# State read-out by matmuls of 65 columns, out of a copy of x with ones between pairs of tiles

## The chip, the cores and the metric

The kernel runs on one core of a Trainium2 chip. The core has five engines with queues of their own: TensorE (PE, matrix multiply, writes to PSUM), VectorE (DVE), ScalarE (ACT), GpSimd (POOL, which also issues DMAs) and SyncE (SP, DMAs only). The metric is device time in microseconds; before the change it is 156.49 us, the median of 6 runs (155.84 to 157.29).

## What is computed

x is (8 batches, 8 heads, 512 positions, 64), state is (8, 8, 32, 64). Two attentions are read in both directions, joined, and put through a feed-forward layer that takes the largest of three products:

```python
scores = scale * x @ state.T;   a  = softmax(scores);   xread = a @ state      # 512 x 64 per head
scores2 = scale * state @ x.T;  a2 = softmax(scores2);  sread = a2 @ x         # 32 x 64 per head
y = concatenate([xread, sread], axis=2)                  # (8, 8, 544, 64)
y = y.transpose(0, 2, 1, 3).reshape(8 * 544, 512)
h = maximum(maximum(y @ w1, y @ w2), y @ w3)             # 4352 x 768
out = h @ w_out                                          # 4352 x 512, float32
```

The softmax subtracts the row's largest score in the reference; the kernel leaves that out. scores2 is the transpose of scores, so one exponential `e` serves both directions: `a` is `e` divided by its sums over the 32 states, and sread is e.T @ x divided by the sums of `e` over the 512 positions.

## The kernel before

All data is bfloat16 on chip, sums are float32 in PSUM. A batch's 512 positions lie on 128 partitions with J = 4 positions each, so that `x_sb[b]` is [128, 8 heads x 4 x 64] and, before the change, has 64 further columns that GpSimd sets to one (lines 66, 114 and 441).

For each batch there are these steps. `x_transpose` or `x_transpose_dma` turns x over (TensorE for batches 0 to 2, DMA transposes issued by SP for 3 to 7). `scores` (L196) multiplies it by a block-diagonal form of the states, and ScalarE's exponential gives `e` (L201). `softmax` sums and inverts on VectorE (L209, L211) and multiplies on GpSimd (L216) to give `a`, which is turned over again into `aT` (SP's DMA transpose, L232, from batch 3). `g_front` and `g_back` (L276) multiply the states by the weights w1, w2, w3 into `G`. `x_maxout` (L348 for the matmuls, L352 to L356 for ScalarE's copy and VectorE's two maxima) makes h from `G` and `aT`, and `ffn_out` (L386) multiplies by w_out; ScalarE copies to `osb` (L389) and GpSimd issues the output DMA in two halves (L400).

`sread(b)` is 32 matmuls (L246), for each of 4 positions j, 2 head groups g and 4 heads s. The stationary operand is a [128, 32] slice of `e`, the moving one has 128 columns: 64 of x and then the 64 columns of ones, one access pattern with a jump (L244). The four s go to four 32-column tiles of the array, which write four groups of 32 PSUM partitions. The result, [128, 2, 2, 64] in one PSUM bank, holds the weighted sums and 64 equal copies of the sum of `e`. VectorE takes the reciprocal of one of the copies (L251) and multiplies (L253) into `sr`; SP transposes that by DMA into `ats` later (L254), for the states' own maxout behind the last batch.

PSUM is held by two rings: "two" (two buffers of two banks: pg pieces and ps) and "pw" (four buffers of one bank: pw, po, psr, pgs and others). Each engine works strictly in the order in which the kernel's text gives it instructions; there is no scheduler. Batches 0 and 1 and part of 2 are written out by hand. From then on one loop pass per b (2 to 7) has six slots, one after each of the six `x_maxout(b, m)`, and the steps of the next batch n = b + 1 are spread over them:

```python
            slots[1].append(lambda: softmax(n, 0, 2, (nc.gpsimd.tensor_mul, J)))
            slots[2].append(lambda: a_transpose_dma(n))
        ...
            slots[4].append(lambda: sread(n))
            slots[4].append(lambda: g_front(n))
```

`ffn_out(b - 1, j)` stands in slots 1, 2, 4 and 5; in slot 4 it comes ahead of sread. sread(2) stands in the part by hand, between `ffn_out(0, 1)` and `g_front(2)`.

Of the kernel before, what the change touches and what calls it, by code (L numbers as in the profile page):

```python
# [8 lines left out]
F32 = mybir.dt.float32  # L9
BF16 = mybir.dt.bfloat16  # L10
AX = mybir.AxisListType
# [4 lines left out]
def kernel(  # L16
# [14 lines left out]
    nc = tc.nc  # L31

    B, H, S, D = x.shape
# [8 lines left out]
    J = 4  # L42
    HS = H // 2
    NM = d_ff // 128
    XW = H * J * D
# [3 lines left out]
    data = ctx.enter_context(tc.tile_pool(name="data", bufs=1))  # L49
    wpool = ctx.enter_context(tc.tile_pool(name="weights", bufs=1))  # L50
    work = ctx.enter_context(tc.tile_pool(name="work", bufs=2))
    pp = ctx.enter_context(tc.tile_pool(name="pp", bufs=2, space=bass.MemoryType.PSUM))
# [10 lines left out]
    load_st(0, nc.sync)  # L63


    x_sb = [data.tile([128, XW + D], BF16, name=f"x{b}") for b in range(B)]
    xv = [t[:, 0:XW].rearrange("p (h j d) -> p h j d", j=J, d=D) for t in x_sb]

    def load_x(b):
        nc.gpsimd.dma_start(  # L70
            out=x_sb[b][:, 0:XW].rearrange("p (h jd) -> p h jd", h=H),
            in_=x[b].rearrange("h (p j) d -> p h (j d)", j=J))
# [26 lines left out]
    def m_cols(t, m):  # L99
        c = [m0 <= m < m1 for m0, m1 in chunks].index(True)  # L100
        f = (m - chunks[c][0]) * 128
        return w_slices(t, c)[:, :, :, f:f + 128]
# [31 lines left out]
    def states_cast(k, cast):  # L134
        cast(out=st[k], in_=st_f[k].unsqueeze(2).to_broadcast((128, 4, 2, D)))
# [19 lines left out]
    def states(k, copy):  # L155
        states_transpose(k, False)
        states_place(k, copy)


    xT, e, a, aT, G, ht, osb = {}, {}, {}, {}, {}, {}, {}  # L160

    def new(d, b, shape, name, bufs=2):
        d[b] = work.tile(shape, BF16, tag=name, bufs=bufs, name=name)
# [16 lines left out]
    def x_transpose_dma(b):  # L180
        new(xT, b, [128, H, 2, 128], "xT", bufs=3)
        nc.sync.dma_start_transpose(out=xT[b].rearrange("p h j t -> p (h j) t"), in_=x_sb[b][:, 0:XW])

    def scores(b, g0, g1):
        n = g1 - g0
        if g0 == 0:
            new(e, b, [128, J, 2, HS, Ns], "e")
        if n == 2:
            p = pp.tile([128, J, n, HS, Ns], F32, tag="two", name="ps")
        else:  # L190
            p = pp.tile([128, J, n, HS, Ns], F32, tag="pw", bufs=4, name="psh")
        for jj in range(2):
            for g in range(g0, g1):
                for s in range(HS):
                    h = 2 * s + g
                    nc.tensor.matmul(  # L196
                        p[:, 2 * jj:2 * jj + 2, g - g0, s, :], xT[b][:, h, jj, :],
                        bd(b, h).rearrange("p c n -> p (c n)"),
                        start=(g == g0 and s == 0 and (n == 2 or jj == 0)),
                        stop=(g == g1 - 1 and s == HS - 1), skip_group_check=True)  # L200
        nc.scalar.activation(out=e[b][:, :, g0:g1], in_=p, func=AF.Exp, scale=scale)  # L201

    def softmax(b, g0, g1, *parts):

        n = g1 - g0
        if g0 == 0:
            new(a, b, [128, J, 2, HS, Ns], "a")
        den = work.tile([128, J, n, HS], F32, tag=f"den{n}", name="den")
        nc.vector.reduce_sum(out=den, in_=e[b][:, :, g0:g1], axis=AX.X)  # L209
        rden = work.tile([128, J, n, HS], F32, tag=f"rden{n}", name="rden")  # L210
        nc.vector.reciprocal(out=rden, in_=den)  # L211
        j0 = 0
        for mul, nj in parts:
            r = slice(j0, j0 + nj)
            j0 += nj
            mul(  # L216
                out=a[b][:, r, g0:g1].rearrange("p j g s n -> p j (g s) n"),
                in0=e[b][:, r, g0:g1].rearrange("p j g s n -> p j (g s) n"),
                in1=rden[:, r].rearrange("p j g s -> p j (g s)").unsqueeze(3).to_broadcast((128, nj, n * HS, Ns)))
# [10 lines left out]
    def a_transpose_dma(b):  # L230
        new(aT, b, [128, J, 2, 128], "aT", bufs=3)
        nc.sync.dma_start_transpose(  # L232
            out=aT[b].rearrange("p j g t -> p (j g) t"), in_=a[b].rearrange("p j g s n -> p (j g s n)"))

    late = []

    def sread(b):

        p = pp.tile([128, 2, 2, D], F32, tag="pw", bufs=4, name="psr")
        for j in range(J):  # L240
            for g in range(2):
                for s in range(HS):
                    xj = xv[b][:, 2 * s + g, j, :]
                    both = bass.AP(xj.tensor, xj.offset,  # L244
                                   (xj.ap[0], (XW - ((2 * s + g) * J + j) * D, 2), (1, D)))
                    nc.tensor.matmul(  # L246
                        p[32 * s:32 * s + 32, g], e[b][:, j, g, s, :], both,
                        start=(j == 0 and g == 0), stop=(j == J - 1), skip_group_check=True,
                        tile_position=(0, 32 * s))
        rd = work.tile([128, 2, 1], F32, tag="rd", name="rd")  # L250
        nc.vector.reciprocal(out=rd, in_=p[:, :, 1, 0:1])  # L251
        sr = work.tile([128, 2, D], BF16, tag="sr", bufs=B, name="sr")
        nc.vector.tensor_mul(out=sr, in0=p[:, :, 0, :], in1=rd.to_broadcast((128, 2, D)))  # L253
        late.append(lambda: nc.sync.dma_start_transpose(  # L254
            out=ats[:, b].rearrange("p s n -> p (s n)"), in_=sr.rearrange("p g d -> p (g d)")))

# [58 lines left out]
    def g_front(b):  # L315
        flush_copies()
        g_piece(b, 0, 512, act)
        g_piece(b, 512, 1024, act, True)
        g_piece(b, 1024, 1280, dve)

    def g_back(b):
        flush_copies()
        g_piece(b, 1280, 1792, act)
        g_piece(b, 1792, 2304, act, True)
# [16 lines left out]
    def maxout(b, m, n, lhs, rhs, nk):  # L341
        if m == 0:
            new(ht, b, [128, NM, n], "ht", bufs=4)
        pw = []
        for i in range(3):
            p = pp.tile([128, 512], F32, tag="pw", bufs=4, name=f"pw{i}")
            for k in range(nk):
                nc.tensor.matmul(p[:, 0:n], lhs(i, k), rhs(k), start=(k == 0), stop=(k == nk - 1))  # L348
            pw.append(p)
        t0 = work.tile([128, 512], BF16, tag="t0", name="t0")  # L350
        t1 = work.tile([128, 512], BF16, tag="t1", name="t1")
        nc.scalar.copy(out=t0[:, 0:n], in_=pw[0][:, 0:n])  # L352
        if copies_due:
            copies_due.pop(0)()
        nc.vector.tensor_max(t1[:, 0:n], t0[:, 0:n], pw[1][:, 0:n])  # L355
        nc.vector.tensor_max(ht[b][:, m, :], t1[:, 0:n], pw[2][:, 0:n])  # L356

    def x_maxout(b, m):
        maxout(b, m, 512,
               lambda i, k: m_cols(G[b], m)[:, k, i],  # L360
               lambda k: aT[b][:, :, k, :], 2)

    def s_maxout(m):
        maxout("s", m, B * Ns,
               lambda i, k: m_cols(w_sb, m)[:, k, i],
               lambda k: ats[:, :, k, :], HS)
# [70 lines left out]
        load_st(k, nc.gpsimd)  # L437
    load_x(3)
    load_x(4)
    for b in range(2, B):  # L440
        nc.gpsimd.memset(x_sb[b][:, XW:XW + D], 1.0)
    for k in range(1, B // 2):
        nc.gpsimd.memset(bds[k], 0.0)
    g_cols(0, (1,))
# [14 lines left out]
    x_maxout(1, 2)  # L459
    for k in range(1, B // 2):  # L460
        states_cast(k, pool)
    x_maxout(0, 4)
    states(1, act)
    x_transpose(2, 0, dve)
# [27 lines left out]
    for b in range(2, B):  # L492
        n = b + 1
        slots = [[] for _ in range(NM)]
        if n < B:
            slots[0].append(lambda: scores(n, 0, 2))
            slots[1].append(lambda: softmax(n, 0, 2, (nc.gpsimd.tensor_mul, J)))
            slots[2].append(lambda: a_transpose_dma(n))
            if n + 2 < B:
                slots[2].append(lambda: x_transpose_dma(n + 2))  # L500
            slots[5].append(late_transposes)
            if n + 3 < B:
                slots[0].append(lambda: load_x(n + 3))
        else:
            for m in range(NM):
                slots[m].append(lambda m=m: s_maxout(m))
        slots[1].append(lambda: g_back(b))
        if n < B:
            slots[4].append(lambda: sread(n))
            slots[4].append(lambda: g_front(n))  # L510
        for j, m in enumerate((1, 2, 4, 5)):
            slots[m].insert(0 if m > 2 else len(slots[m]), lambda j=j: ffn_out(b - 1, j))
        for m in range(NM):
            x_maxout(b, m)
            for f in slots[m]:
                f()
# [36 lines left out]
```

## Time and profile before

| what | value |
|---|---|
| median of 6 runs | 156.49 us (155.84 to 157.29) |
| the profiled execution's own time | 156.25 us |
| its span, first to last instruction | 154.4 us |
| TensorE busy, its granted clock | 147.1 us (95%), 1.00 |
| VectorE, ScalarE, GpSimd busy | 96.3, 94.8, 54.3 us |
| sread matmuls (L246) | 256, of 128 columns, in eight bursts of 32 |
| reciprocal L251, multiply L253 | 161 and 292 ns each, 8 of each |

A row of the groups reads: line, engine, operation, what it writes and reads, shapes, count, then busy us and mean ns of one, then the engine's idle time just before them and what ended it. A timeline or chain line begins with start and length in us, and ends with a count where equal instructions are merged. Busy times of TensorE overlap: a matmul's bar is its latency (219 ns for 128 columns), and the distance from one start to the next is what it costs in a stream.

### The profile page before, as it was taken

How to read it: one execution, taken by the hardware profiler on the slowest of the kernel's cores; microseconds unless marked ns; L12 is line 12 of the kernel's file. 1: busy time of each engine (PE TensorE's matmuls, PEld its weight loads, DVE VectorE, ACT ScalarE, POOL GpSimd, SP SyncE). 2: the span in 40 equal slices, each digit the busy share in tenths (PEclk: the TensorE clock that was granted, in tenths of full speed). 3: DMA queues.
4: the chain of work that ended last, by engine and by line, in shares of the span. 5: the costliest groups of instructions: out<-in, count | busy, mean ns of one | idle time of the engine just before them, and what ended most of it. 6: DMA issues, size and time to landing. Idle time of an engine off the chain costs nothing.

```text
span 154.4 us, 3492 instructions
## 1 busy us (share of the span) xinstructions
PE 147.1 (95%) x1390; PEld 71.9 (47%) x1390; DVE 96.3 (62%) x171; ACT 94.8 (61%) x147; POOL 54.3 (35%) x77
## 2 busy tenths in 40 slices
PE   6899899999999999999999999999999999999980
PEld 2456333454453445344534453445444655566440
DVE  3488776858637666766676667666766675565010
ACT  3667678885768566856685668566856555433350
POOL 8989989023990603060106010601060100101050
PEclk9999999999999999999999999999999999999999
DMA  4999999999699994959511961162115210300465
GB/s 113 219 183 171 177 213 202 236 188 177 89 150 339 203 270 118 149 115 248 119 63 36 225 164 63 66 152 81 59 70 142 84 56 0 138 0 0 185 198 165
DMA packets 36736, 21.72 MB, mean 141 GB/s; under 512 B 21968, under 2 KB 34384, under 8 KB 36720
## 3 DMA queue, kind: packets, MB, share of 16 engines
q0 software_dynamic: 17232, 15.08, 50.1%
q1 hardware_dynamic: 19344, 6.29, 21.9%
q8 instruction: 11, 0.18, 0.5%
q10 hardware_dynamic: 144, 0.13, 0.2%
q14 instruction: 5, 0.04, 0.1%
HBM read 15.20 MB, written 8.91 MB: 156 GB/s over the span
## 4 chain that ended last, share of the span: by engine, by line
PE 87%; DVE 5%; DMA 3%; ACT 1%; issue 1%; SPq 0%; DVEq 0%
PE pw L348 43%; PE po L386 28%; PE pg L276 4%; DMA x0f<-in_x_dram 3%; PE psr L246 2%; PE pxt L174 2%; PE ps L196 2%; PE idle L126 1%; DVE ht L356 1%; DVE t L355 1%; PE pg L302 1%; PE ph L378 1%; ACT t L352 1%; PE psh L196 1%; DVE xT L178 0%
## 5 line engine op out<-in xcount | busy, mean ns | idle before, releaser
L348 PE MATMUL pw<-aT,G 128*128 128x512 bf16 x288 | 69.5, 380 | 0.8 <-DVE sr L253 0.4
L355 DVE TENSOR_TENSOR t<-t,pw 128x512 bf16<-128x512 bf16 (+1 forms) x54 | 35.0, 649 | 30.5 <-ACT t L352 30.5
L386 PE MATMUL po<-wout,ht 128*128 128x512 bf16 x198 | 47.4, 380 | 0.2 <-DVE t L355 0.2
L348 PEld LDWEIGHTS <-G 128*128 128x128 bf16 x288 | 26.8, 98 | 33.3 <-issue 3.8
L356 DVE TENSOR_TENSOR ht<-t,pw 128x512 bf16<-128x512 bf16 (+1 forms) x54 | 35.6, 659 | 5.6
L389 ACT COPY osb<-po 128x512 f32<-128x512 f32 x33 | 19.2, 585 | 29.7 <-PE po L386 28.1
L352 ACT CAST t<-pw 128x512 bf16<-128x512 f32 (+1 forms) x54 | 30.5, 566 | 8.9 <-PE pw L348 7.9
L386 PEld LDWEIGHTS <-ht 128*128 128x128 bf16 x198 | 18.8, 98 | 23.9 <-issue 2.8
L400 POOL DMA_DIRECT2D out_dram<-osb x14 | 7.8, 560 | 55.3 <-ACT osb L389 45.9
L283 ACT CAST G<-pg 128x1024 bf16<-128x1024 f32 x24 | 24.5, 1022 | 3.6 <-PE pg L276 3.1
L216 POOL TENSOR_TENSOR a<-e,rden 128x1024 bf16<-128x1024 bf16 (+2 forms) x10 | 15.3, 1536 | 29.5 <-ACT t L352 15.4
L209 DVE TENSOR_REDUCE den<-e 128x32 f32<-128x1024 bf16 (+1 forms) x10 | 9.9, 995 | 0.7 <-ACT e L201 0.7
L308 ACT CAST G<-pg 128x768 bf16<-128x768 f32 x11 | 8.7, 810 | 2.0 <-PE pg L302 1.9
L109 POOL DMA_DIRECT2D w<-in_moe_w_dram x12 | 9.0, 787 | 0.0
L348 PE MATMUL pw<-ats,w 128*128 128x256 bf16 x72 | 8.8, 273 | 0.0
L201 ACT ACTIVATE e<-ps 128x1024 bf16<-128x1024 f32 x6 | 6.2, 1031 | 3.7 <-PE ps L196 3.7
L348 PEld LDWEIGHTS <-w 128*128 128x128 bf16 x72 | 7.0, 98 | 2.1
L276 PE MATMUL pg<-w,bd 64*32 64x512 bf16 x192 | 7.5, 382 | 0.0
L126 PE MATMUL idle<-zero 128*128 128x512 bf16 x20 | 6.2, 451 | 1.2 <-DVE zero L85 1.2
L196 PEld LDWEIGHTS <-xT 128*128 128x128 bf16 x128 | 5.0, 98 | 2.2 <-DVE xT L178 0.2
L70 POOL DMA_DIRECT2D x<-in_x_dram x6 | 5.4, 908 | 0.8 <-DMA w<-in_moe_w_dram 0.7
L286 DVE CAST G<-pgs 128x256 bf16<-128x256 f32 x12 | 4.5, 419 | 1.1 <-PE pgs L276 1.1
(55 smaller groups left out, 82.7 us busy)
## 6 DMA issues: line engine op xcount, KB each, us to landing
out_dram<-osb POOLq DMA_DIRECT2D x14, 512.0 KB, 3.5
x<-in_x_dram POOLq DMA_DIRECT2D x6, 512.0 KB, 8.9
w<-in_moe_w_dram POOLq DMA_DIRECT2D x6, 256.0 KB, 7.2
x<-in_x_dram POOLq DMA_DIRECT2D x3, 256.0 KB, 5.4
w<-in_moe_w_dram POOLq DMA_DIRECT2D x6, 128.0 KB, 5.8
wout<-in_moe_w_out_dram POOLq DMA_DIRECT2D x1, 768.0 KB, 11.3
x0f<-in_x_dram SPq DMA_DIRECT2D x1, 512.0 KB, 3.9
out_dram<-osb SPq DMA_DIRECT2D x1, 512.0 KB, 2.6
```

The costliest lines, as they stand in the source:

```text
L109: nc.gpsimd.dma_start(out=w_slices(w_sb, c)[:, :, i, :], in_=w[:, :, m0 * 128:m1 * 128])
L196: nc.tensor.matmul(p[:, 2 * jj:2 * jj + 2, g - g0, s, :], xT[b][:, h, jj, :], bd(b, h).rearrange("p c n -> p (c n)"), start=(g == g0 and s ...
L209: nc.vector.reduce_sum(out=den, in_=e[b][:, :, g0:g1], axis=AX.X)
L216: mul(out=a[b][:, r, g0:g1].rearrange("p j g s n -> p j (g s) n"), in0=e[b][:, r, g0:g1].rearrange("p j g s n -> p j (g s) n"), in1=rden[: ...
L276: nc.tensor.matmul(ps[g][32 * s:32 * s + 32], bd(b, 2 * s + g)[64 * g:64 * g + 64, g, :], w_sb[64 * g:64 * g + 64, s, c0:c1], start=True, ...
L283: copy(out=G[b][:, :, c0:c1], in_=p[:, :, 0:n])
L348: nc.tensor.matmul(p[:, 0:n], lhs(i, k), rhs(k), start=(k == 0), stop=(k == nk - 1))
L352: nc.scalar.copy(out=t0[:, 0:n], in_=pw[0][:, 0:n])
L355: nc.vector.tensor_max(t1[:, 0:n], t0[:, 0:n], pw[1][:, 0:n])
L356: nc.vector.tensor_max(ht[b][:, m, :], t1[:, 0:n], pw[2][:, 0:n])
L386: nc.tensor.matmul(p, ht[b][:, m, j * 128:(j + 1) * 128], wout_sb[:, m, :], start=(m == 0), stop=(m == NM - 1))
L389: act(out=o[:, j, :], in_=p)
```

## The change

For batches 2 to 7 sread reads another layout. Two buffers `x_pads` hold, for each pair of 64-wide tiles (one head, two positions j), two ones and then the pair's 128 columns, 130 in all, with two more ones at the very end. The ones are set once. `x_pad(b)` is one GpSimd copy of all of x's 2048 columns into buffer b % 2. It is issued for batch 2 after the states' casts in the part by hand, and for n = b + 1 in slot 1 behind the softmax of n.

A matmul now moves 65 columns. For even j it is one of the ones and the first tile of a pair, into PSUM columns 0 to 64; for odd j it is the second tile and the following one, into columns 1 to 65. So x's sums fall on columns 1 to 64 for both, and the sum of `e` comes in two parts, in columns 0 and 65, which VectorE adds with a reduce ahead of the reciprocal. The slices for even j begin at an odd element. Batches 0 and 1 keep the 128 columns. The ones behind x_sb[2] to x_sb[7], and the six memsets that made them, are gone.

```diff
-    x_sb = [data.tile([128, XW + D], BF16, name=f"x{b}") for b in range(B)]
+    x_sb = [data.tile([128, XW + D if b < 2 else XW], BF16, name=f"x{b}") for b in range(B)]
...
+    PW = 2 * D + 2
+    x_pads = [data.tile([128, (2 * H + 1) * PW], BF16, name=f"xp{k}") for k in range(2)]
+
+    def x_pad(b):
+        nc.gpsimd.tensor_copy(
+            out=x_pads[b % 2][:, 2:2 + 2 * H * PW].rearrange("p (k c) -> p k c", c=PW)[:, :, 0:2 * D],
+            in_=x_sb[b][:, 0:XW].rearrange("p (k c) -> p k c", c=2 * D))
+
     def sread(b):
-        p = pp.tile([128, 2, 2, D], F32, tag="pw", bufs=4, name="psr")
+        padded = b >= 2
+        p = pp.tile([128, 2, 2 * D], F32, tag="pw", bufs=4, name="psr")
         for j in range(J):
             for g in range(2):
                 for s in range(HS):
-                    xj = xv[b][:, 2 * s + g, j, :]
-                    both = bass.AP(xj.tensor, xj.offset,
-                                   (xj.ap[0], (XW - ((2 * s + g) * J + j) * D, 2), (1, D)))
+                    h = 2 * s + g
+                    if padded:
+                        c0 = (2 * h + j // 2) * PW + 1 + (D + 1) * (j % 2)
+                        cols = x_pads[b % 2][:, c0:c0 + D + 1]
+                        c = slice(j % 2, D + 1 + j % 2)
+                    else:
+                        xj = xv[b][:, h, j, :]
+                        cols = bass.AP(xj.tensor, xj.offset, (xj.ap[0], (XW - (h * J + j) * D, 2), (1, D)))
+                        c = slice(0, 2 * D)
                     nc.tensor.matmul(
-                        p[32 * s:32 * s + 32, g], e[b][:, j, g, s, :], both,
+                        p[32 * s:32 * s + 32, g, c], e[b][:, j, g, s, :], cols,
                         start=(j == 0 and g == 0), stop=(j == J - 1), skip_group_check=True,
                         tile_position=(0, 32 * s))
+        den, c = p[:, :, D:D + 1], slice(0, D)
+        if padded:
+            den, c = work.tile([128, 2, 1], F32, tag="rs", name="rs"), slice(1, D + 1)
+            nc.vector.reduce_sum(out=den, in_=p[:, :, 0:D + 2:D + 1], axis=AX.X)
         rd = work.tile([128, 2, 1], F32, tag="rd", name="rd")
-        nc.vector.reciprocal(out=rd, in_=p[:, :, 1, 0:1])
+        nc.vector.reciprocal(out=rd, in_=den)
         sr = work.tile([128, 2, D], BF16, tag="sr", bufs=B, name="sr")
-        nc.vector.tensor_mul(out=sr, in0=p[:, :, 0, :], in1=rd.to_broadcast((128, 2, D)))
+        nc.vector.tensor_mul(out=sr, in0=p[:, :, c], in1=rd.to_broadcast((128, 2, D)))
...
-    for b in range(2, B):
-        nc.gpsimd.memset(x_sb[b][:, XW:XW + D], 1.0)
+    for t in x_pads:
+        nc.gpsimd.memset(t.rearrange("p (k c) -> p k c", c=PW)[:, :, 0:2], 1.0)
...
     for k in range(1, B // 2):
         states_cast(k, pool)
+    x_pad(2)
     x_maxout(0, 4)
...
             slots[1].append(lambda: softmax(n, 0, 2, (nc.gpsimd.tensor_mul, J)))
+            slots[1].append(lambda: x_pad(n))
             slots[2].append(lambda: a_transpose_dma(n))
```

## The prediction

> **What bounds the kernel now.** I read the page's first part and the chain that ended last, then the chain piece by piece over one pass of the loop.
>
> ```profile
> span 154.4 us, 3492 instructions
> PE 147.1 (95%) x1390; PEld 71.9 (47%) x1390; DVE 96.3 (62%) x171; ACT 94.8 (61%) x147; POOL 54.3 (35%) x77
> ...
> PE 87%; DVE 5%; DMA 3%; ACT 1%; issue 1%; SPq 0%; DVEq 0%
> ...
> 69.33 1.29 PE po L386 x6
> 70.62 0.56 PE psr L246 x32
> 71.18 0.56 PE pg L276 x16
> 71.74 0.11 PE pgs L276 x8
> 71.84 1.40 PE pw L348 x6
> ```
>
> TensorE is the bound. From about 47 us on the chain is TensorE and nothing else, in passes of 15.4 us (the sread pieces begin at 55.21, 70.62, 86.03, 101.44, 116.84). What leaves TensorE in this stretch leaves the span. One sread is 0.56 of a pass, and six of the eight sreads (batches 2 to 7) are changed: 3.36 us in all is what the change can act on.
>
> Next, what the 0.56 us is made of. The timeline of TensorE cut off at four moments shows how many of the 32 matmuls have started, and the last two lines, from a whole-burst view, give the scores' matmuls of 64 columns, which are the nearest row to 65.
>
> ```profile
> 70.55 0.24 PE L246 MATMUL psr<-x,e 128*32 128x128 bf16 x4
> 70.55 0.29 PE L246 MATMUL psr<-x,e 128*32 128x128 bf16 x8
> 70.55 0.35 PE L246 MATMUL psr<-x,e 128*32 128x128 bf16 x12
> 70.55 0.41 PE L246 MATMUL psr<-x,e 128*32 128x128 bf16 x16
> ...
> 75.67 0.63 PE L196 MATMUL ps<-bd,xT 128*128 128x64 bf16 x16
> 76.14 0.38 PE L348 MATMUL pw<-aT,G 128*128 128x512 bf16 x1
> ```
>
> Four matmuls (one for each 32-column tile of the array) run side by side, and each further four add 0.057: 8 rounds of 0.056 to 0.057 = 0.45. The other 0.11 is filling and emptying the array where the tile shape changes; it stays. A round is 128 columns: 0.44 ns a column. The scores' 16 matmuls take 76.14 - 75.67 = 0.47 us, 29 ns each for 64 columns: 0.46 ns a column. So short matmuls still go by columns at half the length.
>
> Last, GpSimd's own timeline in this pass, and its rows of comparable work.
>
> ```profile
> 65.74 1.90 POOL L216 TENSOR_TENSOR a<-e,rden 128x1024 bf16<-128x1024 bf16 x1 [4.25 <-DVE rden L211]
> 67.65 0.61 POOL L400 DMA_DIRECT2D out_dram<-osb  x1
> 75.46 0.53 POOL L400 DMA_DIRECT2D out_dram<-osb  x1 [7.20 <-ACT osb L389]
> ...
> L152 POOL COPY bd<-stT 64x512 bf16<-64x512 bf16 x4 | 4.3, 1072 | 0.2
> L443 POOL MEMSET bd<- 128x1024 bf16 x3 | 2.8, 970 | 0.0
> L135 POOL CAST st<-stf 128x512 bf16<-128x512 f32 x3 | 1.8, 616 | 3.5 <-DMA stf<-in_state_dram 3.5
> ```
>
> It is idle for most of each pass, but the new copy is queued directly behind `a`, which ends at 67.65, and the sread that needs the copy begins at 70.55. That leaves 2.9 us.
>
> **The change, part by part.**
>
> *The matmuls (removed columns).* 65 columns for 128. At the scores' rate a round of 65 is 29.4 + 0.4 = 30 ns; 8 rounds 0.24, with the unchanged 0.11: 0.35 for 0.56. Gain 0.21 a sread, six times 1.26 us. Against it stands a rule of the Trainium skill, "TensorE: Matmul & The Clock Gate", Part 3, "What overlaps and what doesn't": weight loads overlap with running matmuls only where the row groups differ. All tiles here use all 128 rows, so by that rule each round would also pay for its load, which the page puts at columns / 1.2 ns, 27 ns for 32: 57 ns a round, no gain. The row decides: the scores' matmuls use all rows, each has its own load, and still start every 29 ns. An sread's load is of 32 columns only; the first four matmuls last 230 ns where later ones last 219, so an uncovered load costs about 12 ns, which fits under 30. I take 0.35; bounds: 0.56 (no gain: loads, or a penalty of moving slices that begin on an odd element, of which no row exists) and 0.32 (the changeovers shrink a little too). Batch 2's sread is followed by a wait on ScalarE (the chain has ACT t at 39.61, then DVE t), but that chain starts from the cast of the pg piece that follows the sread, so it comes 0.21 earlier too, and the gain stands.
>
> *The copy on GpSimd (added, six).* 128x2048, one input, unit steps in runs of 128. The cast (512 elements, one input, unit steps, 616 ns) is the nearest row. Times four it is 2.46; with about 0.1 of it fixed (a 128x64 memset shows 170 ns, 85 from start to start) 2.1 to 2.2. The memset's slope, (970 - 170) / 960 = 0.83 ns an element, gives a floor of 1.8; L152's copy, with the same opcode that this one will have but reading with a step of 256 bytes, gives 4 x 1.07 = 4.3. I take 2.1. The Trainium skill speaks against it: "GPSIMD Engine Reference", section 7, counts 1.9 cycles an element as the good case and 2.9 with a wide step. At 1.2 GHz that is 3.24 us for 2048. The cast's 616 ns is 1.44 cycles an element with all overhead in, so here the page is too dear, and I keep the row. By the row: ready at 67.6 + 2.1 = 69.7, 0.8 us ahead of the sread, cost nothing. By the page: 70.9, 0.35 late, five times = 1.7, and the sum would be +0.45 instead of -1.26. The cover that hides the copy is the 2.9 us of maxout and output matmuls between `a` and sread; beyond it each us of the copy costs five (batch 2's copy stands in the idle stretch from 31.8 to 37.1 and has 5 us).
>
> *What is queued behind the copy on GpSimd.* The first half of a batch's output DMA, issued at 67.65 today, now about 69.7. Its osb buffer is one of two and is written again two passes later, so nobody waits. The second half (75.46) and the load of x at the pass's start come before the next `a` or long after the copy. `a` itself is ahead of the copy, and so is SP's transpose of `a` (67.67, lands 4.7 us later, needed near 74.4). The copy waits for x's load, which the transposes of the same x needed long before, and for the sread two batches back. Cost 0.
>
> *VectorE.* A reduce of 128x2x2 before the reciprocal: L251's reciprocal of 128x2 is 170 ns, so about 0.17 plus 0.03 of waiting, 0.20. Late behind it: the reciprocal, sr, the two pgs casts, and through sr the PSUM buffer that the second pw tile takes. Today sr ends at 71.73 and that pw tile starts at 72.2. Now the sread ends 0.21 earlier and the reduce takes 0.20 back: sr ends at 71.73 still, the pw tile starts at 71.99, 0.26 to spare; the pgs casts leave about 0.2. Cost 0; if the reduce were 0.4 instead, about 0.2 a sread would come back.
>
> *Memsets.* Six of 64 elements (0.6 us in all) leave GpSimd near 23.3 and two of 17x2 enter; GpSimd then waits for state's DMA until 30.6 anyway. 0. TensorE's first sread matmul waits for GpSimd where it waited for another engine: one wait for another, 0.
>
> **Sum.** The profiled execution was 156.25 us: 154.4 of span and 1.85 around it. 154.4 - 1.26 = 153.14, with 1.85 it is 154.99. The median of the runs shown, 156.49, is 0.24 above the profiled one: 155.2 predicted.
>
> **Rivals.**
> *The copy is late* (ends slower). Place: the first matmul of sread, waiting for GpSimd. For it: L152's row (4.3 us) and the page's 3.2. Against: L152 reads with a wide step and this copy doesn't. It eats the gain from 2.9 + 1.26/5 = 3.15 us on and is over 0.5% slower (0.78 us more) from 3.3 us. At 4.3 us it is 1.4 late, five times 7.0 less 1.26: 162.2.
> *TensorE doesn't go by columns here.* For it: 8 instructions of 7 ns each in a round today would have to come at 3.7 ns; the odd start of half the slices. Against: instructions within a round start 2 to 4 ns apart. Full loss: 156.5; half: 155.9.
> *VectorE takes it back.* If the pw or po tile after sread waits for the later sr or casts: up to 0.2 a pass, 156.2. Against: the slack worked out above.
>
> **How the numbers follow.** Likeliest case 0.60 (its own range 154.8 to 155.6). TensorE gains half or nothing 0.17 (155.7 to 156.7). VectorE gives some back 0.04. Copy late but under 3.3 us 0.06 (155.3 to 157.2), beyond 3.3 us 0.13 (157.3 to 162.5). Half a per cent, 0.78 us, is about what a measurement of this kernel tells from no change. Faster by more than that (below 155.7): 0.60 and 0.02 of the mixed cases; slower (above 157.3): 0.13 and 0.02 for what isn't named; same 0.23. The range leaves out the long tail of the late copy above and little below: 154.7 to 157.4.
>
> **What would show it.** Right: psr pieces of 0.35 in the chain, passes of 15.2, the GpSimd copy at 1.8 to 2.5 us, ended before sread, no wait of psr on GpSimd, output DMA issues at about +2 us. Wrong: psr still 0.5 or more, or TensorE idle before psr with GpSimd's copy as releaser, or a new idle before pw released by VectorE.

## The result

The changed kernel takes 155.24 us (median) against 156.56 us for the kernel before: a ratio of 0.9914, 95% interval 0.9897 to 0.9931. That is 1.35 us less, 1.08 to 1.61. 155.2 had been predicted.

The ratios compare undisturbed executions alone, and since the first profile of the changed kernel was of a disturbed one (161.0 us span, in which TensorE waited 3.6 us for two late landings of `aT`), the lines here are from a second execution, labelled after_again below. First its chain over one pass of the loop, to be laid beside the five chain lines of before.

```profile
69.87 1.29 PE po L407 x6
71.17 0.36 PE psr L263 x29
71.53 0.56 PE pg L297 x16
72.08 0.11 PE pgs L297 x8
72.19 1.40 PE pw L369 x6
```

Only the sread piece has changed, from 0.56 to 0.36 us. (Three of its 32 matmuls are missing from the record.) The matmul groups have new line numbers: L263 is sread, L297 the G pieces, L369 and L407 the maxout and the output.

Next, the timeline of TensorE cut off at four moments, as it was for the kernel before.

```profile
71.10 0.21 PE L263 MATMUL psr<-xp,e 128*32 128x65 bf16 x4
71.10 0.25 PE L263 MATMUL psr<-xp,e 128*32 128x65 bf16 x8
71.10 0.28 PE L263 MATMUL psr<-xp,e 128*32 128x65 bf16 x12
71.10 0.31 PE L263 MATMUL psr<-xp,e 128*32 128x65 bf16 x16
...
71.09 0.31 PEld L263 LDWEIGHTS <-e 128*32 128x32 bf16 x32 [0.42 <-issue]
```

Four more matmuls now add 0.03 to 0.04 us, where they added 0.057. From round to round the starts in the trace are 39, 36, 29, 35, 29, 31 and 29 ns apart; before it was 67 and then 55 to 57. The last line, from a view of the whole burst, has its weight loads: all 32 lie in 0.31 us, beside the matmuls and not between them.

GpSimd's timeline in the same pass, and the groups of the two operations that were added:

```profile
66.28 1.91 POOL L216 TENSOR_TENSOR a<-e,rden 128x1024 bf16<-128x1024 bf16 x1 [4.25 <-DVE rden L211]
68.14 1.88 POOL L242 COPY xp<-x 128x2048 bf16<-128x2048 bf16 x1
69.98 0.61 POOL L421 DMA_DIRECT2D out_dram<-osb  x1
...
L242 POOL COPY xp<-x 128x2048 bf16<-128x2048 bf16 x6 | 11.3, 1882 | 0.0
L270 DVE TENSOR_REDUCE rs<-psr 128x2 f32<-128x4 f32 x6 | 1.0, 160 | 1.5 <-PE psr L263 1.5
```

The copy ends at 70.02 and sread begins at 71.10: it has 1.08 us to spare. The reduce's 1.5 us of idle time is VectorE waiting for the matmuls, which is nobody's loss.

The two profiled executions have the same span, 154.4 us, although one kernel is faster. A span contains the start, where the first loads land earlier or later: sread of batch 0 begins at 14.3 us in the execution of before and at 15.3 in this one. It contains the end too, the 4.0 and 4.2 us behind the chain's last ScalarE copy (oh). From the start of sread(2) to the start of sread(7) it is 37.66 to 116.78 before, 79.12 us, and 38.60 to 116.73 after, 78.14. The five passes hold 0.98 us less, 0.197 each, which is the psr piece's 0.560 - 0.363. From the start of sread(7) to the end of that ScalarE copy it is 33.66 and 33.46 us, so the sixth sread brings as much. Six make 1.18 us, inside the interval of the measured gain.

### The profile page after: what moved, and what is told of

It reads as the page before. It is cut to its first block, busy times and chain, and to the rows that moved or that the text cites. A ratio compares the mean times of both kernels' runs of the same rounds, so it can differ in the third digit from the quotient of the medians.

```text
span 161.0 us, 3499 instructions
## 1 busy us (share of the span) xinstructions
PE 148.8 (92%) x1390; PEld 72.0 (45%) x1390; DVE 97.3 (60%) x177; ACT 95.2 (59%) x147; POOL 64.8 (40%) x79
## 4 chain that ended last, share of the span: by engine, by line
PE 59%; DMA 20%; POOL 7%; DVE 6%; ACT 4%; issue 2%; POOLq 0%; DVEq 0%; SPq 0%; ACTq 0%
PE pw L369 32%; PE po L407 17%; DMA aT<-a 10%; DMA stT<-st 5%; DMA x<-in_x_dram 4%; POOL a L216 4%; PE pg L297 2%; DVE den L209 2%; DVE ht L377 2%; PE ps L196 1%; ACT G L329 1%; DVE t L376 1%; POOL bd L152 1%; PE idle L126 1%; ACT t L373 1%
## 5 line engine op out<-in xcount | busy, mean ns | idle before, releaser
L369 PE MATMUL pw<-aT,G 128*128 128x512 bf16 x288 | 70.8, 385 | 4.3 <-DMA aT<-a 3.6
L407 PE MATMUL po<-wout,ht 128*128 128x512 bf16 x198 | 47.4, 380 | 0.2 <-DVE t L376 0.2
L369 PEld LDWEIGHTS <-G 128*128 128x128 bf16 x288 | 26.9, 99 | 37.9 <-issue 7.9
L407 PEld LDWEIGHTS <-ht 128*128 128x128 bf16 x198 | 18.8, 98 | 23.9 <-issue 2.8
L216 POOL TENSOR_TENSOR a<-e,rden 128x1024 bf16<-128x1024 bf16 (+2 forms) x10 | 15.3, 1535 | 28.6 <-PE pw L369 10.3
L242 POOL COPY xp<-x 128x2048 bf16<-128x2048 bf16 x6 | 11.3, 1882 | 0.0
L369 PE MATMUL pw<-ats,w 128*128 128x256 bf16 x72 | 8.8, 273 | 0.0
L126 PE MATMUL idle<-zero 128*128 128x512 bf16 x20 | 7.1, 501 | 1.2 <-DVE zero L85 1.2
L369 PEld LDWEIGHTS <-w 128*128 128x128 bf16 x72 | 7.0, 98 | 2.1
L297 PE MATMUL pg<-w,bd 64*32 64x512 bf16 x192 | 7.5, 382 | 0.0
L152 POOL COPY bd<-stT 64x512 bf16<-64x512 bf16 x4 | 4.3, 1064 | 6.0 <-DMA stT<-st 5.9
L196 PEld LDWEIGHTS <-xT 128*128 128x128 bf16 x128 | 5.5, 103 | 2.4 <-issue 0.6
```

Source lines behind the costliest of these rows:

```text
L216: mul(out=a[b][:, r, g0:g1].rearrange("p j g s n -> p j (g s) n"), in0=e[b][:, r, g0:g1].rearrange("p j g s n -> p j (g s) n"), in1=rden[: ...
L242: nc.gpsimd.tensor_copy(out=x_pads[b % 2][:, 2:2 + 2 * H * PW].rearrange("p (k c) -> p k c", c=PW)[:, :, 0:2 * D], in_=x_sb[b][:, 0:XW].re ...
L297: nc.tensor.matmul(ps[g][32 * s:32 * s + 32], bd(b, 2 * s + g)[64 * g:64 * g + 64, g, :], w_sb[64 * g:64 * g + 64, s, c0:c1], start=True, ...
L407: nc.tensor.matmul(p, ht[b][:, m, j * 128:(j + 1) * 128], wout_sb[:, m, :], start=(m == 0), stop=(m == NM - 1))
```

## The experiments

The theory: all of the gain is 0.2 us of TensorE a sread, and the copy, the reduce and the output DMA behind the copy are covered. The rivals: a second source of gain or loss in the copy, the DMAs or VectorE.

**The changed kernel again (after_again).**

> The changed kernel once more, for a profile that can be laid beside that of before. My theory (TensorE is the bound, one sread costs 0.36 us of it instead of 0.56, six times, the copy and the reduce are hidden): about 1.2 us under before, 155.3; passes of 15.2 us; GpSimd's copy 1.9 us and done 1 us ahead of sread. Rival (the gain has a second source beside the columns, such as the memsets that left GpSimd or DMAs issued at another time): the span falls by clearly more than six times the difference of the psr pieces.

155.34 us, ratio 0.9927 (0.9901 to 0.9953). The passes are 15.21 us, and the lines above are from it. No second source of gain is needed.

**The columns without the copy (columns_only).**

```diff
-                        c0 = (2 * h + j // 2) * PW + 1 + (D + 1) * (j % 2)
-                        cols = x_pads[b % 2][:, c0:c0 + D + 1]
-                        c = slice(j % 2, D + 1 + j % 2)
+                        c0 = (h * J + j) * D
+                        cols = x_sb[b][:, c0:c0 + D + 1]
+                        c = slice(0, D + 1)
...
-    x_pad(2)
...
-            slots[1].append(lambda: x_pad(n))
```

> 65 neighbouring columns straight out of x_sb, without copy, without ones between pairs, with the memsets of before; the reduce stays. The 65th column is the next tile's first and not a one, so the sums that sread is divided by are left out. My theory: the same 1.2 us under before as the whole change, since the copy costs nothing and the columns are all of the gain. Rival (the copy costs something on VectorE, TensorE or the DMAs): faster than the whole change by 0.3 us or more.

155.28 us, ratio 0.9925 (0.9901 to 0.9949), the whole change's time. Without the ones this kernel divides by wrong sums; what it shows is the time of the narrower matmuls. Its chain has the short sread piece, and its passes are 15.21 us:

```profile
71.09 0.36 PE psr L263 x32
```

So the columns alone give the gain, as far as the interval can tell.

**The copy without the columns (copy_only).**

```diff
-        padded = b >= 2
+        padded = False
```

> The copy and its memsets are made, nobody reads them; sread moves 128 columns as before and has no reduce. My theory: as before, within 0.3 us (GpSimd has the time, and what is queued behind it isn't due). Rival (the later output DMA or the copy's traffic costs something): slower than before by 0.3 us or more.

156.53 us, ratio 1.0004 (0.9977 to 1.0032). GpSimd's timeline has the copy in the same place, behind `a`:

```profile
66.08 1.91 POOL L216 TENSOR_TENSOR a<-e,rden 128x1024 bf16<-128x1024 bf16 x1 [4.25 <-DVE rden L211]
67.94 1.88 POOL L242 COPY xp<-x 128x2048 bf16<-128x2048 bf16 x1
69.77 0.61 POOL L421 DMA_DIRECT2D out_dram<-osb  x1
```

The passes are 15.41 us, as in the kernel before. So 11.3 us of added GpSimd work cost nothing that can be measured (the interval allows 0.5 us), and neither does the output DMA that is issued 1.8 us later.

**How much cover the copy has (copy_twice).**

```diff
     def x_pad(b):
-        nc.gpsimd.tensor_copy(
+        for _ in range(2):
+            nc.gpsimd.tensor_copy(
```

> The changed kernel with each copy of x made twice, one behind the other. In the profile of the changed kernel the copy takes 1.84 us from start to start and ends at 70.0 where sread begins at 71.1. My theory (2.9 us of cover behind the multiply, then each us of the copy costs five): the second copy ends 0.8 us late in batches 3 to 7, TensorE waits for GpSimd ahead of sread there, 4.0 us in all, about 159.3. Batch 2 waits for nothing. Rival (TensorE has slack elsewhere in a pass that takes up the wait): less than 2 us over the changed kernel.

159.94 us, ratio 1.0213 (1.0151 to 1.0274), 4.6 us above the 155.34 of after_again. The chain of this kernel shows what took over:

```profile
66.95 1.91 POOL a L216
68.86 1.84 POOL xp L243
70.70 0.05 issue
70.75 1.91 POOL xp L243
72.66 0.04 issue
72.70 0.43 PE psr L264 x32
```

and its list of waits has the price:

```profile
PE psr L264 <- POOL xp L243: 4.2, 5, 0.9
```

Five waits, none for batch 2, as expected. A pass grows from 15.21 to 16.14 us, 0.93, and five passes give 4.65. The 4.0 us expected was a little low: the second copy ends 1.96 us behind the first, not 1.84. The list has 4.2 us and not 4.65 because it counts from the end of the last matmul's bar, which outlasts sread's start by 0.07 us where nothing is late (0.38 against 0.31 us from start to start). The cover is real, and behind it the copy costs what it is late, five times. Nothing else in a pass takes the wait up.

**How much VectorE has to spare behind sread (reduce_five).**

```diff
-            nc.vector.reduce_sum(out=den, in_=p[:, :, 0:D + 2:D + 1], axis=AX.X)
+            for _ in range(5):
+                nc.vector.reduce_sum(out=den, in_=p[:, :, 0:D + 2:D + 1], axis=AX.X)
```

> The changed kernel with the new reduce issued five times instead of once. Four more of them are 0.4 to 0.65 us, as they follow each other at 0.1 to 0.16. My theory (0.22 us between sr's end and the matmul that takes its PSUM buffer): TensorE waits 0.2 to 0.4 us for VectorE's sr behind each of the six sreads, 1.2 to 2.4 us in all. Rival (VectorE's 37% of idle time takes it up): no more than 0.3 us.

158.23 us, ratio 1.0111 (1.0054 to 1.0169), 2.9 us above after_again: the mechanism of the theory, and more of it than I had said. The chain of this kernel runs through VectorE behind sread (shortened), and the waits name the link:

```profile
72.08 0.41 PE psr L263 x29
...
72.51 0.17 DVE rs L271
72.68 0.02 issue
72.70 0.17 DVE rs L271
...
73.69 0.30 DVE sr L275
73.99 0.05 issue
74.03 1.04 PE pw L370 x4
...
PE pw L370 <- DVE sr L275: 2.4, 6, 0.4
```

The reduces follow each other at 0.195 us, not 0.1 to 0.16 (they write the same tile, which may be why; no run tried it otherwise). Four more are 0.78. A pass grew to 15.78 us, 0.57 more, so 0.21 of the 0.78 was hidden. This 0.21 is what VectorE has to spare behind sread, as worked out from the buffers; its idle 37% over the whole span says nothing about it.

**The odd start of half the slices (even_start).**

```diff
-                        c0 = (2 * h + j // 2) * PW + 1 + (D + 1) * (j % 2)
-                        cols = x_pads[b % 2][:, c0:c0 + D + 1]
-                        c = slice(j % 2, D + 1 + j % 2)
+                        c0 = (2 * h + j // 2) * PW + (D + 2) * (j % 2)
+                        cols = x_pads[b % 2][:, c0:c0 + D + 2]
+                        c = slice(2 * (j % 2), D + 2 + 2 * (j % 2))
```

> 66 columns a matmul with both ones of a gap, so that every slice begins on an even element; the two halves of the sum land in columns 0 and 66. If the odd start of half the slices costs something, psr pieces fall below 0.363 us and the steps from round to round, which alternate between 29 and 35 ns, become even. If not (what I expect): psr 0.363 + 8 x 0.4 ns = 0.366, time as the changed kernel.

155.29 us, ratio 0.9915 (0.9891 to 0.9940). The psr pieces are 0.361 to 0.365 us (0.362 to 0.366 with the odd starts), and the steps alternate as there (39, 36, 29, 33, 30, 34, 29 ns). So the odd start costs nothing that shows. Behind the first, the longer steps are those to the next position j, where the columns that are written shift. In columns_only, where they don't shift, the steps are 39, 36, 29, 30, 29, 29 and 35 ns and the piece is 0.356 to 0.358 us. What makes a step longer isn't settled.

**The copy one slot earlier (copy_early).**

```diff
+            slots[0].append(lambda: x_pad(n))
             slots[1].append(lambda: softmax(n, 0, 2, (nc.gpsimd.tensor_mul, J)))
-            slots[1].append(lambda: x_pad(n))
```

> The changed kernel with the copy of batches 3 to 7 one slot earlier, ahead of the softmax multiply in GpSimd's queue instead of behind it. GpSimd is idle there, so my theory is the same time as the changed kernel within 0.3 us, with the copy done 4 us or more ahead of sread. Rival (the copy pushes the multiply back, and through SP's transpose of its result the next pass): slower by up to 1 us, with the multiply starting later in the pass than 3.6 us after the scores.

156.32 us, ratio 0.9965 (0.9935 to 0.9995): by the medians 1.0 us of the gain is gone, by the ratios (0.9927 for after_again) 0.6, which I had not expected. It isn't the rival that I named, since `a` starts in its place (66.15 us, where the changed kernel has 66.28), and the profiled execution shows passes of 15.21 us and no wait. That execution took 155.25 us, though, and so is one that lost nothing. In GpSimd's queue two things moved beside the copy: the load of x three batches ahead (batches 6 and 7) now stands behind the copy, and the first half of the output DMA is again issued right behind `a`.

**The load ahead of the early copy (copy_early_load_first)**, only the order of these two in slot 0 changed:

```diff
             if n + 3 < B:
                 slots[0].append(lambda: load_x(n + 3))
...
+            slots[0].append(lambda: x_pad(n))
             slots[4].append(lambda: sread(n))
```

> As the kernel with the copy one slot earlier, but with the load of x three batches ahead issued before the copy and not behind it. The early copy came out 1 us slower than the changed kernel although its profiled execution had passes of 15.2 us without a wait. If the loads of batches 6 and 7, 1.8 us later there, are the cause: back to the changed kernel's time within 0.4 us. If it is the copy's place ahead of the multiply, or the first half of the output DMA that is issued 1.8 us earlier than in the changed kernel: again about 1 us slower.

155.45 us, ratio 0.9925 (0.9891 to 0.9959). To see if this was chance, both kernels ran once more on one chip, with a third that makes the loads late and nothing else.

> The kernel with the early copy once more, on the same chip as the next two. If its 1 us was real: again between before and the changed kernel, near 156.3. If it was chance: about 155.4 like the kernel with the load first.

> The early copy with the load ahead of it once more. 155.4 again by the reading that the load's place makes the difference; by chance alone no different from the one before it.

copy_early_2: 156.45 us, ratio 0.9953 (0.9912 to 0.9993). load_first_2: 155.26 us, ratio 0.9894 (0.9842 to 0.9946). The difference came again, 0.9 us by the ratios, though the intervals still touch.

**The load alone made late (load_delayed).**

```diff
+                slots[0].append(lambda: nc.gpsimd.memset(idle_t, 0.0))
                 slots[0].append(lambda: load_x(n + 3))
```

> The changed kernel, its copy where it was, with a GpSimd memset of 128x2048 (1.7 us) ahead of the loads of x for batches 6 and 7 and of nothing else. If a load issued 1.8 us later costs about 1 us: near 156.3. If it doesn't: 155.3, and the early copy lost its time by something else.

154.93 us, ratio 0.9898 (0.9854 to 0.9941). My reading fell: a late load alone costs nothing. In this kernel the output DMA stands behind the copy, though, and in copy_early it doesn't. The second profile of the early copy (copy_early_2) shows who can be hurt by the two together. These are the lines on batch 3's `aT`, for which TensorE waited:

```profile
L232 SPq DMA_TRANSPOSE aT<-a x1: 1244/1244/1244, 53.3 to 53.3; - x1
  DMA aT<-a: 0.2, 1
DMA to landing us min/median/max: 6.5/6.5/6.5
```

A late landing of this one is no mark of the early copy by itself: in the two kernels with the load first it takes 5.9 and 6.2 us, and in load_delayed 6.0, and TensorE waits for none of these.

**Early copy, output DMA late again (early_out_late).**

```diff
             slots[1].append(lambda: softmax(n, 0, 2, (nc.gpsimd.tensor_mul, J)))
+            slots[1].append(lambda: nc.gpsimd.memset(idle_t, 0.0))
```

> The kernel with the early copy (load behind it), plus a GpSimd memset of 128x2048 (1.7 us) behind the softmax multiply, where the changed kernel has its copy: the first half of the output DMA is again issued 1.7 us later than SP's transpose of a. In the profiles so far that transpose lands in 3.2 us where the output DMA comes later (changed kernel, delayed load) and in 4.6 us where both are issued together (before, early copy), and in the second profile of the early copy batch 3's landed after 6.5 us, and TensorE waited for it. If the early copy's loss comes from the output DMA and the late load meeting that transpose: back to 155.3, transpose in 3.2 us. If not: again near 156.3.

155.37 us, ratio 0.9922 (0.9893 to 0.9951). By the medians the early copy loses its 1 us only where both hold: the load late and the output DMA issued along with SP's transpose of `a`. Either undone brings the time back. The intervals overlap (0.9893 to 0.9951 here, 0.9935 to 0.9995 for the early copy), so this is likely and not shown. Through which wait the time goes is only partly seen. In copy_early_2's profile `aT` of batch 3 comes late and that pass is 15.58 us instead of 15.21, 0.37 of about 1 us; batch 3's `aT` also took 5.8 us in early_out_late's profile, without a wait there. The rest of the loss is in executions that were not profiled, and stays open.

## Why the prediction was right

**TensorE is the bound, and what leaves it leaves the span**: right. columns_only and copy_only split the change in two, and all of the gain is on TensorE's side.

**The matmuls.** 0.35 us was predicted for an sread, 0.363 was measured, so 1.18 us for six instead of 1.26. The term that was a little off is the round, 30 ns by the scores' row; the rounds take 29 to 36, with one of 39 at the start. The rule of the Trainium skill that spoke against the change ("TensorE: Matmul & The Clock Gate", Part 3, loads overlap only where the row groups differ) would have given rounds of 57 ns, by an estimate that adds the page's load time; here every tile uses all 128 rows, rounds of 29 ns occur, and the 32 loads lie beside the matmuls, so loads overlap there too. The scores' row was the better guide, though it is a full-array burst and sread runs in four tiles. Of a penalty for an odd start, kept open then, nothing shows (even_start).

**The copy.** 2.1 us was taken from the cast, 1.88 was measured, 1.84 from start to start: 0.90 ns an element, close to the memset's slope (0.83). The 1.9 cycles an element of the Trainium skill's "GPSIMD Engine Reference", section 7, an estimate of 3.24 us at 1.2 GHz, is too dear for this plain copy with unit steps: the measured 1.84 us is 1.08 cycles by the same clock. The L152 row, with the same opcode, costs 2.1 ns an element; its wide step is the likely reason, but no run tried it. The cover of 2.9 us and the factor of five behind it held to a tenth (copy_twice), so the main rival was a matter of the copy's size alone. At the page's price the copy would have ended at 71.4 us and been late.

**What is queued behind the copy.** No cost, as predicted (copy_only). But "nobody waits" was not the whole truth: the place of that DMA changes how fast SP's transposes land, as the last section shows.

**VectorE.** 0.20 us was predicted for the reduce with its wait; it is 160 ns and 35 of waiting. The slack of 0.2 to 0.26 held: 0.21 by reduce_five. One sentence of the prediction was too dear: it let a reduce of 0.4 us give 0.2 back, but the 0.2 more is just what is hidden.

**The sum.** The profiled executions could not have shown the gain by their spans; the median does, and it stands 0.04 from the prediction. This closeness is partly luck, since the gain itself is known to a quarter of a microsecond.

## What to carry to other kernels

Where one engine is the whole chain, count the starts of its instructions within a burst: what a round costs, and what of the burst is a fixed changeover, tells what a shorter operand will save. Work for an idle engine is free up to the first consumer that waits for it, and then, here, costs its lateness times the passes; measure that cover in the trace ahead of adding the work, and the slack of each buffer behind it, since an engine's mean idle time tells neither. And look at what a copy pushes back in its queue: a DMA that is issued later or earlier meets other DMAs.

## What was not expected of the hardware

An output DMA of 512 KB issued by GpSimd at the same moment as SP's DMA transpose made that transpose slower here. For batches 4 to 7 the landing of `aT` reads, in the kernel before and then in the changed one, where that output DMA comes 1.8 us later:

```profile
DMA to landing us min/median/max: 3.8/4.6/4.9
```

```profile
DMA to landing us min/median/max: 3.1/3.2/3.2
```

SP's next issue, the transpose of x behind it, shows the same; these are the lines of one pass. In the kernel before, and then in the changed one:

```profile
69.02 3.77 SPq L182 DMA_TRANSPOSE xT<-x  x1
```

```profile
69.56 1.56 SPq L182 DMA_TRANSPOSE xT<-x  x1
```

It follows the DMA and not the rest of the change: copy_only and early_out_late, with the late output DMA, have medians of 3.1 and 3.2 us for the same batches, and the early copy 4.6. columns_only, which has the gain and no copy, has 4.5. Batch 3's transpose, which is issued 3 to 7 us after a load of x, takes 3.7 to 6.5 us in the profiles of all the runs, whenever that output DMA comes; why wasn't tested. In the two profiles compared here TensorE doesn't wait for either transpose, so the shorter landing buys nothing; it shows that the change also moved a transfer out of another's way.
